# The head of a sketched-attention and ELU kernel: z's sums ahead of the query sketches, the first key transpose ahead of the mask product, one query load

## The chip, the cores and the metric

The kernel runs on one core of a Trainium2 chip. The metric is the device time of one execution, in microseconds (us). Engines are named as the profile names them: PE is the matrix engine (PEld its weight loads), DVE the vector engine, ACT the scalar engine, POOL the GpSimd engine, SP the sync engine, which here only issues DMAs. A "q" behind an engine's name (SPq, ACTq) means its instruction queue, where DMAs are issued.

## The reference

q, k and v are (4, 4, 1088, 32): batch, heads, rows, head size. S1 and S2 are two 8 x 32 sketch matrices.

```
phi(x)  = outer product of (S1 x) and (S2 x), 8 x 8 = 64 features per row
kv      = sum over rows of phi(k) v^T          (64 x 32 per batch and head)
z       = sum over rows of phi(k)              (64 per batch and head)
x       = (phi(q) kv) / (phi(q) z + 1e-6)      -> (4352, 128), heads side by side
h       = x @ w_in                             (128 -> 2048)
out     = elu(h) @ w_out                       (2048 -> 128)
```

The sketches and both weight matrices arrive as 64-bit floats and are rounded to 32 bits on the chip with integer operations (`round_a` to `round_e`). Everything else is 32-bit float.

## The kernel before

**Tiling.** The 1088 rows of a batch are 17 tiles of 64 rows. Keys are handled as two halves u = 0 and 1 of at most nine tiles each (`KT` is 9), which lie in the two halves of the partitions of a result; products for both halves can run side by side in the matrix engine. The 68 tiles of queries are taken in groups of eight tiles (512 rows). Group 0 is the first 512 rows of batch 0, and the head of the kernel is what must happen before group 0 can go through the two large matrix products: sketch the keys of batch 0, build kv and z from them, sketch and normalise the queries of group 0.

**Order.** The schedule is written by hand: each engine executes its instructions in the order of the program text, and an instruction that waits holds all that stand behind it on its engine. Tiles come from rotating buffers, and waits are put in by the framework where data or buffers need them. DMAs are issued from SP and, for the first loads, from ACT. From the ninth on, an issue on SP also waits until an earlier DMA, eight places before it in the order of all issues, has landed.

**The head, in order** (lines of the profile in brackets):

- SP and ACT each load one sketch [L139] and one part of batch 0's keys: SP tiles 0 to 8, ACT tiles 9 to 16, both through `load_hd` [L78]. Then each loads half of group 0's queries [L78 again, called from L144 and L145]. SP goes on with the first weight block [L164], v [L86], the other queries, more weights.
- PE runs `keep_warm` products, whose result is never read [L231]; then the mask product's input `sps` [L265] and `SXps` [L251], then one more unread product with 224 columns [L231].
- DVE multiplies `sps` with a head mask into `Sab`, the sketch matrix spread over heads [L268], and then transposes the keys in four pieces [L244]: tiles 0 to 4 (from SP's load), 9 to 13 (from ACT's load), 5 to 8, 14 to 16. After them come the queries of group 0 [L244].
- `KF(0)`: 18 products of key tiles with `Sab` into two PSUM banks `abp` [L304], and one ACT copy of each bank into `abk` [L312]. The first bank needs tiles i below 5 of both halves, the second the rest.
- `q1_first`: 8 products with the transposed queries, `abqp` [L482], copied by ACT to `abq` [L486].
- `KO_pool` and `KO_first`: the outer products `kp`. POOL makes tiles 0 to 3 [L287], DVE tile 4 and, in one instruction of 1024 elements per partition, tiles 5 to 8 [L374].
- `Z_first`: nine products that sum z over the tiles, `zps` [L382; tiles 0 to 4 need `abk`'s first copy, 5 to 8 its second], an ACT copy `zl` [L404], two products with the masked sketches `SXh` [L226], a DVE mask product that writes the third part of `SW` [L413], and an unread product of 160 columns [L231].
- `q1z_first`: 8 products of the queries with that part of `SW`, `zqp` [L494], which are the queries' denominators before the last reduction.
- `RA(0)` [L103, DVE]: the first step of rounding weight block 0. `RB(0)` is ACT's step of it [L108].
- `q2_den`: DVE multiplies, sums, inverts and scales: `pw` [L569], `den` [L572, L573], `an` [L575]. `q2_out` writes `qp` in two instructions [L586].
- `KA(0)`: 36 products `kv` [L391], and the chain that turns them [L446 to L448]. Then `qp` is transposed on PE [L598], copied by ACT [L599], multiplied with kv [L605], copied to `xg` [L611].
- `mm1_first` and what follows are the first of the large products, `h` [L226], ELU [L791, L793, L799] and `o` [L226], with the rounding of the next weight blocks in between on DVE [L103, L116, L117, L121, L129].

Each product in 32-bit floats is run by PE as two passes, so 18 products show as 36.

From step 2 on a loop over 68 (group, weight block) pairs issues the two large products of each, with the work of the other three batches placed at given steps.

Of the kernel before, what the change touches and what calls it, by code (L numbers as in the profile page):

```python
# [22 lines left out]
def _ap(ap: bass.AP, free):  # L23
    return dataclasses.replace(ap, ap=[list(ap.ap[0])] + [list(x) for x in free])
# [3 lines left out]
def kernel(  # L28
# [21 lines left out]
    nc = tc.nc  # L50
# [7 lines left out]
    NT = S // 64  # L58
    KT = (NT + 1) // 2
# [12 lines left out]
    kT = [const.tile([FD, 2 * KT, 64], F32, name=f"kT{b}") for b in range(2)] * 2  # L72
    qT = [const.tile([FD, NT, 64], F32, name=f"qT{b}") for b in range(2)] * 2

    def load_hd(eng, x, src, b, t0, t1, c=slice(0, 2)):
        if (x, b) not in hd:
            hd[x, b] = work.tile([P, 2, NT, D], F32, name="hd_" + x, tag="hd_" + x)
        eng.dma_start(hd[x, b][:, c, t0:t1, :],  # L78
                      src[b].rearrange("h (a c t) d -> (h a) c t d", a=32, c=2)[:, c, t0:t1, :])
# [61 lines left out]
            eng.dma_start(S16[rs, :], src)  # L141
    load_hd(nc.sync, "k", k, 0, 0, KT)
    load_hd(nc.scalar, "k", k, 0, KT, NT)
    load_hd(nc.sync, "q", q, 0, 0, 8, slice(0, 1))  # L144
    load_hd(nc.scalar, "q", q, 0, 0, 8, slice(1, 2))  # L145
    warm = const.tile([R, 1], F32, name="warm")
    nc.vector.memset(warm[:], 0.0)
    nc.scalar.activation(warm[:], warm[:], EXP)
# [75 lines left out]
    def halves(dst, lhs, rhs, **kw):  # L224
        for u in range(2):
            nc.tensor.matmul(dst[64 * u:64 * u + 64], lhs[:, 64 * u:64 * u + 64], rhs, skip_group_check=True,  # L226
                             tile_position=(0, 64 * u), **kw)

    def keep_warm(n, cols=256):
        for i in range(n):  # L230
            nc.tensor.matmul(idle[:, :cols], some[:, :P], some[:, :cols], skip_group_check=True)  # L231
# [11 lines left out]
    def transp(dst, x, b, t0, t1):  # L243
        nc.vector.transpose(dst[b][:, t0:t1, :].rearrange("p t (a c) -> p c t a", c=2), hd[x, b][:, :, t0:t1, :])  # L244
# [4 lines left out]
    def make_SXh():  # L249
        xps = psum.tile([P, 512], F32, name="SXps", tag="aux")  # L250
        nc.tensor.matmul(xps[:, :FD], idr[:].rearrange("p x j -> p (x j)"), Sx[:].rearrange("p h d -> p (h d)"))  # L251
        nc.scalar.copy(SXh[:], xps[:, :FD])
        nc.gpsimd.tensor_mul(SXh[:].rearrange("p (h d) -> p h d", h=H), SXh[:].rearrange("p (h d) -> p h d", h=H),
                             _ap(hmask[:], [[1, H], [0, D]]))
# [9 lines left out]
    sps = psum.tile([P, 512], F32, name="sps", tag="aux")  # L264
    nc.tensor.matmul(sps[:, :2 * R], Sx[:].rearrange("p h d -> p (h d)"), ident[:, :2 * R])  # L265
    make_SXh()
    keep_warm(1, 224)
    nc.vector.tensor_mul(Sab[:], _ap(sps[:, :2 * R], [[0, H], [1, 2 * R]]), _ap(bmask[:], [[1, H], [0, 2 * R]]))  # L268
    nc.gpsimd.tensor_copy(SW[:, :, :2, :].rearrange("p h x r -> p h (x r)"), Sab[:])

# [26 lines left out]
    def KF(b):  # L297
        ps = [psum.tile([P, 512], F32, name="abp", tag="h", bufs=4) for _ in range(2)]

        part = [(range(5), 0), (range(3), 1)]  # L300
        todo = [(i, u) for r, u in part for i in r] + [x for i in range(5, KT) for x in ((i - 2, 1), (i, 0))]
        todo += [(i, 1) for i in range(KT - 2, KT)]
        for i, u in todo:
            nc.tensor.matmul(ps[i // 5][64 * u:64 * u + 64, 64 * (i % 5):64 * (i % 5) + 64],  # L304
                             kT[b][:, u * KT + i, :], Sab[:].rearrange("p h y -> p (h y)"),
                             skip_group_check=True, tile_position=(0, 64 * u))
        kf_ps.extend(ps)
        ab = feats[b] = work.tile([P, 2, KT, H, R], F32, name="abk", tag="abk", bufs=2)
        for j in range(2):
            t = slice(0, 5) if j == 0 else slice(5, KT)  # L310
            n = t.stop - t.start
            nc.scalar.copy(ab[:, :, t].rearrange("p x t h r -> p x (t h) r"),  # L312
                           ps[j][:, :64 * n].rearrange("p (m x r) -> p x m r", x=2, r=R))
# [49 lines left out]
    def KO_pool():  # L363
        for half in range(2):
            feats[0, half] = work.tile([P, 5, H, R, R], F32, name="kp", tag="kp", bufs=3)
        ab = feats[0][:, :, :4].rearrange("p x t h r -> p (t h) x r")
        outer(feats[0, 0][:, :4].rearrange("p t h i j -> p (t h) i j"), ab, nc.gpsimd)

    def KO_first(t0, t1):
        half, o = divmod(t0, 5)  # L370
        n = t1 - t0
        a_ = kf_ps[half][:, 64 * o:64 * (o + n)].rearrange("p (m x r) -> p m x r", x=2, r=R)[:, :, 1, :]
        b_ = feats[0][:, 0, t0:t1].rearrange("p t h r -> p (t h) r")
        nc.vector.tensor_mul(feats[0, half][:, o:o + n].rearrange("p t h i j -> p (t h) i j"),  # L374
                             _ap(a_, list(a_.ap[1:]) + [[0, R]]), _ap(b_, [[R, n * H], [0, R], [1, R]]))
# [3 lines left out]
    def z_tile(b, ps, i):  # L379
        c = 32 * (i % 4)  # L380
        ab = feats[b]
        nc.tensor.matmul(ps[c:c + 32, R * R:R * R + H * R], ab[:, 0, i].rearrange("p h r -> p (h r)"),  # L382
                         ab[:, 1, i].rearrange("p h r -> p (h r)"), start=(b == 0 and i < 4), stop=(i >= KT - 4),
                         skip_group_check=True, tile_position=(0, c))
# [17 lines left out]
    def ZC(b, ps):  # L402
        zl = work.tile([P, H * R], F32, name="zl", tag="zl")
        nc.scalar.copy(zl[:], ps[:, R * R:R * R + H * R])  # L404
        return zl

    def Z(b, ps, zl):

        halves(ps[:, 96:128], SXh[:], zl[:])

    def Z_out(b, ps):
        z = wzs[b] = SW[:, :, 2, :] if b == 0 else work.tile([FD, H, R], F32, name="wz", tag="wz")[:]
        nc.vector.tensor_mul(z, ps[:, 96:128].rearrange("p (h i) -> p h i", h=H), _ap(bmask[:], [[1, H], [0, R]]))  # L413
# [21 lines left out]
    def Z_first():  # L435
        ps = psum.tile([P, 512], F32, name="zps", tag="h", bufs=4)
        for i in range(KT):
            z_tile(0, ps, i)
        zl = ZC(0, ps)
        Z(0, ps, zl)  # L440
        Z_out(0, ps)
        keep_warm(1, 160)

    def KS_first():
        kd = work.tile([P, 2, R * R], F32, name="kd", tag="kd", bufs=1)
# [18 lines left out]
    def half_tile(g, k):  # L464
        return divmod(8 * g + k, NT)
# [11 lines left out]
    def q1_first():  # L477
        p = psum.tile([P, 512], F32, name="abqp", tag="aux")
        for i in range(4):
            for u in range(2):  # L480
                b, t = half_tile(0, 2 * i + u)
                nc.tensor.matmul(p[64 * u:64 * u + 64, i * 64:i * 64 + 64], qT[b][:, t, :],  # L482
                                 Sab[:].rearrange("p h y -> p (h y)"),
                                 skip_group_check=True, tile_position=(0, 64 * u))
        abw[0] = work.tile([P, H * 4, 2 * R], F32, name="abq", tag="abq", bufs=1)
        nc.scalar.copy(abw[0][:].rearrange("p (h t) y -> p h t y", h=H),  # L486
                       p[:, :256].rearrange("p (t h y) -> p h t y", t=4, h=H))

    def q1z_first():
        p = psum.tile([P, 512], F32, name="zqp", tag="h", bufs=4)  # L490
        for i in range(4):
            for u in range(2):
                b, t = half_tile(0, 2 * i + u)
                nc.tensor.matmul(p[64 * u:64 * u + 64, i * 32:i * 32 + 32].rearrange("p (h r) -> p h r", h=H),  # L494
                                 qT[b][:, t, :], SW[:, :, 2, :], skip_group_check=True, tile_position=(0, 64 * u))
        return p[:, :128].rearrange("p (t h r) -> p h t r", t=4, h=H)
# [349 lines left out]
                eng.dma_start(rows[b, :, t, :], o[64 * u:64 * u + 64, i])  # L846


    for t0, t1 in ((0, 5), (KT, KT + 5), (5, KT), (KT + 5, NT)):
        transp(kT, "k", 0, t0, t1)  # L850
    KF(0)
    transp(qT, "q", 0, 0, 8)
    q1_first()
    KO_pool()
    KO_first(4, 5)
    KO_first(5, KT)
    Z_first()
    zq = q1z_first()
    RA(0)
    q2_den(0, zq)  # L860
# [201 lines left out]
```

## Time and profile before

| | us |
|---|---|
| median of 4 runs | 268.05 |
| lowest and highest of them | 267.55, 268.72 |
| the profiled execution | 267.54 |
| its span, first to last instruction | 265.7 |
| PE busy in it | 259.6 (98%) |
| DVE, ACT, POOL busy | 187.5, 184.0, 159.8 |

The span is counted from the first instruction; about 1.8 us of the execution lie around it. An engine counts as busy from the start to the (for PE modelled) end of its instructions. The waits of an engine are put down to the instruction that released it.

### The profile page before, as it was taken

The page shows a single profiled execution, that of the slowest core. Times are in us where ns is not written, and L with a number is a line of the kernel's source. Part 1 is how long each engine was busy: PE and PEld are TensorE (multiplying, and loading weights), DVE is VectorE, ACT ScalarE, POOL GpSimd, SP SyncE. Part 2 cuts the span into 40 slices and gives each one's busy share as a digit, 9 for nine tenths or more (in the row PEclk, how much of TensorE's full clock was granted, in tenths as well). Part 3 has the DMA queues.
Part 4 walks back from the last instruction along what each step waited for, and adds up shares of the span by engine and source line. Part 5 has one row for each costly group of instructions (what it writes and reads, how often), then busy time and mean ns, then how long its engine had stood idle before and what let it go on. Part 6 is the DMA issues. An engine that isn't in the chain of part 4 may idle for free.

```text
span 265.7 us, 7686 instructions
## 1 busy us (share of the span) xinstructions
PE 259.6 (98%) x3115; PEld 154.4 (58%) x3115; DVE 187.5 (71%) x346; ACT 184.0 (69%) x355; POOL 159.8 (60%) x233
## 2 busy tenths in 40 slices
PE   8899999999999999999999999999999999999994
PEld 6753333343334665668566666666766666666884
DVE  6899999996969796996557766654346444673652
ACT  2379978677566565786577777777777777777782
POOL 4400008204415985798859799898688888898300
PEclk9999999999999999999999999999999999999999
DMA  5999960011002200000100110001000100110011
GB/s 188 316 349 245 272 191 4 0 38 51 0 0 38 47 4 0 2 3 16 28 5 0 22 22 2 0 14 26 9 0 12 31 2 1 18 21 6 2 27 35
DMA packets 26418, 13.60 MB, mean 51 GB/s; under 512 B 19216, under 2 KB 24592, under 8 KB 26384
## 3 DMA queue, kind: packets, MB, share of 16 engines
q1 hardware_dynamic: 25792, 12.66, 18.8%
q8 instruction: 24, 0.39, 0.6%
q10 hardware_dynamic: 592, 0.46, 0.5%
q14 instruction: 10, 0.08, 0.1%
HBM read 10.88 MB, written 2.23 MB: 49 GB/s over the span
## 4 chain that ended last, share of the span: by engine, by line
PE 94%; DVE 4%; issue 1%; ACT 0%; DVEq 0%
PE h L226 43%; PE pb L730 16%; PE pa L730 12%; PE o L226 11%; PE ol L226 3%; PE idle L231 2%; PE kv L391 1%; PE h L648 1%; PE qps L648 1%; DVE qp L586 1%; PE kfps L323 1%; PE qps L542 1%; PE kv L226 1%; PE abp L304 1%; DVE raw L121 0%
## 5 line engine op out<-in xcount | busy, mean ns | idle before, releaser
L799 DVE SCALAR_TENSOR_TENSOR gg<-e,h 128x512 f32<-128x512 f32 (+1 forms) x144 | 92.2, 651 | 64.2 <-ACT e L793 62.9
L226 PE MATMUL h<-xg,W 128*64 128x512 f32 (+1 forms) x584 | 128.7, 563 | 0.0
L791 ACT ACTIVATE e<-h 128x512 f32<-128x512 f32 (+1 forms) x144 | 81.5, 566 | 50.4 <-PE h L226 48.0
L793 ACT ACTIVATE e<-e 128x512 f32<-128x512 f32 (+1 forms) x144 | 87.5, 607 | 4.4
L226 PEld LDWEIGHTS h<-xg,W 128*64 128x64 f32 x584 | 40.1, 137 | 47.4 <-issue 36.8
L710 POOL TENSOR_TENSOR tt<-gg 128x256 f32<-128x256 f32 x48 | 35.2, 732 | 16.4 <-DVE gg L799 16.0
L713 POOL TENSOR_TENSOR tt<-gg 128x256 f32<-128x256 f32 x48 | 35.4, 738 | 14.2 <-DVE gg L799 13.8
L715 POOL TENSOR_TENSOR tt<-gg,tt 128x256 f32<-128x256 f32 x48 | 36.5, 761 | 3.8
L714 POOL TENSOR_TENSOR tt<-tt,gg 128x256 f32<-128x256 f32 x48 | 35.2, 734 | 3.8
L730 PEld LDWEIGHTS pa<-gg,W 128*64 128x64 f32 x384 | 23.6, 137 | 22.8 <-issue 22.1
L226 PE MATMUL o<-gg,W 128*64 128x512 f32 x128 | 30.5, 597 | 0.4 <-DVE W L129 0.4
L730 PE MATMUL pa<-gg,W 128*64 128x128 f32 x384 | 29.5, 274 | 0.0
L730 PE MATMUL pb<-tt,SS 128*64 128x128 f32 x384 | 29.1, 273 | 0.0
L730 PEld LDWEIGHTS pb<-tt,SS 128*64 128x64 f32 x384 | 22.6, 137 | 0.0
L126 POOL TENSOR_TENSOR raw<-raw,tiny 128x512 f32<-128x512 f32 x1 | 1.0, 1047 | 29.9 <-DVE raw L121 29.9
L730 PE MATMUL pb<-gg,SS 128*64 128x128 f32 x192 | 18.7, 273 | 0.0
L730 PE MATMUL pa<-tt,SS 128*64 128x128 f32 x192 | 18.7, 273 | 0.0
L730 PE MATMUL pb<-tt,W 128*64 128x128 f32 x192 | 18.6, 273 | 0.0
L226 PEld LDWEIGHTS o<-gg,W 128*64 128x64 f32 x128 | 8.5, 136 | 16.2 <-issue 13.8
L730 PEld LDWEIGHTS pb<-tt,W 128*64 128x64 f32 x192 | 12.1, 137 | 0.0
L730 PEld LDWEIGHTS pa<-tt,SS 128*64 128x64 f32 x192 | 12.1, 137 | 0.0
L730 PEld LDWEIGHTS pb<-gg,SS 128*64 128x64 f32 x192 | 12.1, 137 | 0.0
(150 smaller groups left out, 243.5 us busy)
## 6 DMA issues: line engine op xcount, KB each, us to landing
raw<-in_moe_w_in_dram SPq DMA_DIRECT2D x8, 256.0 KB, 5.9
raw<-in_moe_w_out_dram SPq DMA_DIRECT2D x8, 256.0 KB, 6.2
hd_k<-in_k_dram SPq DMA_DIRECT2D x3, 544.0 KB, 8.2
hd_q<-in_q_dram SPq DMA_DIRECT2D x3, 544.0 KB, 3.5
v<-in_v_dram SPq DMA_DIRECT2D x4, 288.0 KB, 6.7
out_dram<-ob SPq DMA_DIRECT2D x72, 16.0 KB, 1.5
v<-in_v_dram SPq DMA_DIRECT2D x4, 256.0 KB, 8.2
out_dram<-ob SPq DMA_DIRECT2D x16, 32.0 KB, 1.6
```

What stands on the lines that cost most here:

```text
L226: nc.tensor.matmul(dst[64 * u:64 * u + 64], lhs[:, 64 * u:64 * u + 64], rhs, skip_group_check=True, tile_position=(0, 64 * u), **kw)
L231: nc.tensor.matmul(idle[:, :cols], some[:, :P], some[:, :cols], skip_group_check=True)
L304: nc.tensor.matmul(ps[i // 5][64 * u:64 * u + 64, 64 * (i % 5):64 * (i % 5) + 64], kT[b][:, u * KT + i, :], Sab[:].rearrange("p h y -> p ( ...
L648: nc.tensor.matmul(ps[w][s * r:s * r + s, 64 * k:64 * (k + m)], lhs, qpT[g, i][rows, o + 2 * k:o + 2 * (k + m), f, :], start=(f == 0 and j ...
L710: nc.gpsimd.tensor_tensor(t[:, 0], b12, b11, op=SUB)
L713: nc.gpsimd.tensor_tensor(t[:, 2], b22, b12, op=SUB)
L714: nc.gpsimd.tensor_tensor(t[:, 1], t[:, 2], b11, op=ADD)
L715: nc.gpsimd.tensor_tensor(t[:, 3], b21, t[:, 1], op=SUB)
L730: nc.tensor.matmul(bank[64 * u:64 * u + 64, P * col:P * col + P], lhs, rhs[:, u], start=(first and i in (0, 3)), stop=last, skip_group_che ...
L791: nc.scalar.activation(e, hs[g, cp][c][:, :n], RELU, scale=-1.0)
L793: nc.scalar.activation(e, e, EXP, scale=-1.0)
L799: nc.vector.scalar_tensor_tensor(gs[g, cp][:, c, :n], es[g, cp][:, c, :n], -1.0, hs[g, cp][c][:, :n], op0=ADD, op1=MAX)
```

## The change

Four edits, all in the head:

- the queries of group 0 are loaded whole by one DMA from SP, and ACT issues none for them;
- the transpose of key tiles 0 to 4 stands on DVE ahead of the mask product that makes `Sab`, and the unread product of 224 columns after `SXps` is gone;
- `Z_first` is cut in two. Its nine sums and the copy `zl` stand ahead of `q1_first`, on PE and on ACT; its two products and the mask product stand between the outer products of tiles 5 and 6 and those of tiles 7 and 8, which are now two DVE instructions;
- the unread product after z's products has 96 columns where it had 160.

```diff
-    load_hd(nc.sync, "q", q, 0, 0, 8, slice(0, 1))
-    load_hd(nc.scalar, "q", q, 0, 0, 8, slice(1, 2))
+    load_hd(nc.sync, "q", q, 0, 0, 8)
@@ after make_SXh()
-    keep_warm(1, 224)
+    transp(kT, "k", 0, 0, 5)
     nc.vector.tensor_mul(Sab[:], _ap(sps[:, :2 * R], [[0, H], [1, 2 * R]]), _ap(bmask[:], [[1, H], [0, 2 * R]]))
@@ Z_first
         for i in range(KT):
             z_tile(0, ps, i)
-        zl = ZC(0, ps)
-        Z(0, ps, zl)
-        Z_out(0, ps)
-        keep_warm(1, 160)
+        return ps, ZC(0, ps)
@@ the order of the head
-    for t0, t1 in ((0, 5), (KT, KT + 5), (5, KT), (KT + 5, NT)):
+    for t0, t1 in ((KT, KT + 5), (5, KT), (KT + 5, NT)):
         transp(kT, "k", 0, t0, t1)
     KF(0)
     transp(qT, "q", 0, 0, 8)
+    zps, zl = Z_first()
     q1_first()
     KO_pool()
     KO_first(4, 5)
-    KO_first(5, KT)
-    Z_first()
+    KO_first(5, 7)
+    Z(0, zps, zl)
+    Z_out(0, zps)
+    KO_first(7, KT)
+    keep_warm(1, 96)
     zq = q1z_first()
```

## The prediction

> **What bounds the kernel now.** I read three views of the profiled execution: the page's engine totals, the chain that ended last, and the timeline of the first 22 us.
>
> ```profile
> PE 259.6 (98%) x3115; PEld 154.4 (58%) x3115; DVE 187.5 (71%) x346; ACT 184.0 (69%) x355; POOL 159.8 (60%) x233
> ```
>
> PE is the bound: 98% busy, and in the timeline it never idles after 22.09 us. The first product of `o` there waits for DVE, and before it comes a row of DVE work without holes. The chain that ended last, asked for the first 30 us, shows that row (start, length, what):
>
> ```profile
> 7.53 0.61 PE abqp L482 x16
> 8.16 0.37 ACT abq L486
> 8.54 0.13 ACT zl L404
> 8.80 0.31 PE zps L226 x4
> 9.11 0.47 PE idle L231 x2
> 9.58 0.61 PE zqp L494 x16
> 10.22 0.30 DVE pw L569
> ...
> 11.56 1.29 DVE qp L586 x2
> 12.86 0.69 DVE qT L244
> ...
> 21.61 0.43 DVE W L129
> 22.04 0.04 issue
> 22.09 1.94 PE o L226 x8
> ```
>
> Every piece from 10.22 to 22.04 is DVE's, or a gap of at most 0.1 us between dependent DVE instructions (one piece is booked as "issue" while `qp` still runs). None waits for a DMA. So whatever moves `pw` at 10.22 moves the end by as much. The question is what `pw` waits for, and the timeline answers (start, length, instruction, idle time before it):
>
> ```profile
> 5.08 0.23 DVE L268 TENSOR_TENSOR Sab<-sps,bmask 128x64 f32<-128x64 f32 x1 [0.76 <-PE sps L265]
> 5.39 0.54 PE L231 MATMUL idle<-some 128*128 128x224 f32 x2
> 5.87 1.67 PE L304 MATMUL abp<-Sab,kT 128*64 128x64 f32 x36
> 7.10 0.84 ACT L312 COPY abk<-abp 128x320 f32<-128x320 f32 x2 [1.24 <-PE abp L304]
> 7.44 0.69 PE L482 MATMUL abqp<-Sab,qT 128*64 128x64 f32 x16
> 7.56 1.64 DVE L374 TENSOR_TENSOR kp<-abp,abk 128x256 f32<-128x256 f32 x2 [0.26 <-ACT abk L312]
> 8.06 0.38 PE L382 MATMUL zps<-abk 128*32 128x32 f32 x18
> 8.80 0.31 PE L226 MATMUL zps<-zl,SXh 128*64 128x32 f32 x4 [0.37 <-ACT zl L404]
> 9.22 0.19 DVE L413 TENSOR_TENSOR SW<-zps,bmask 128x32 f32<-128x32 f32 x1
> 9.51 0.66 PE L494 MATMUL zqp<-SW,qT 128*64 128x32 f32 x16
> 10.22 0.29 DVE L569 TENSOR_TENSOR pw<-abq,zqp 128x128 f32<-128x128 f32 x1 [0.51 <-PE zqp L494]
> ```
>
> Read backwards: `pw` waits for `zqp`, `zqp` for `SW`. `SW` has two conditions that come almost together: z's products end at 9.11, and DVE is held by `kp` until 7.56 + 1.64 = 9.20. `kp` wins by some 0.05 us. This closeness decides the forecast.
>
> **The change part by part.** Times below are of the profiled execution, 267.54 us for a span of 265.7, which is 0.5 us under the median 268.05 of the runs.
>
> *The key transposes.* The first needs SP's key load: issued at 1.20, and the DMA list gives 3.7 us to landing, so 4.90. DVE idles 0.76 us before `Sab`, so the transpose starts near 4.92 and, at its 0.50 us, ends at 5.42. Consecutive DVE instructions here start some 0.08 us before their predecessor ends, so `Sab` moves from 5.08 to 5.35 and ends at 5.57, not 5.31. DVE is then free for the second transpose at 5.49, against 5.65 before. But that one reads ACT's load: issued at 1.37, 4.2 us to landing, 5.57. It starts near 5.60, a gain of 0.05. The bounds are 0.16 (landing earlier) and a loss of 0.14, the row of `Sab`'s 0.23 less the overlap, when SP's load lands after 5.2 and `Sab` is held behind a transpose that waits. I take 0.05, by the landing rows.
>
> *The key sketches.* The 18 passes of half u = 1 follow the second transpose 0.15 us behind and 0.058 apart, so they end the sketches. The first sketch, now behind `Sab`, starts at 5.71 instead of 5.87, and is no limit. Both `abk` copies come 0.05 earlier; the second ends at 7.89 (was 7.10 + 0.84 = 7.94).
>
> *z's sums ahead of `abqp`.* This looks like the gain and is not one. The sums of tiles 5 to 8 need the second `abk` copy; they started 0.12 behind it before (8.06) and do so after (8.01). What changes is PE's order: `abqp` ran at 7.44 to 7.96 while PE would have waited for that copy; now it is queued behind the waiting sums. It starts when their last eight passes are through (0.08) and PE has changed to 64-column tiles (0.15, as from `zqp` to `kv` the other way): 8.24. Its 16 passes hold PE for 0.52 us, to 8.76. Meanwhile ACT has made `zl` by 8.52, as no `abq` copy stands ahead of it, and z's products could start 0.14 later, at 8.66. They start at 8.76, behind `abqp`: against 8.80 a gain of only the 0.05 from above. Were the tile change free they would start at 8.66; were it 0.15 longer, at 8.91.
>
> *The outer products cut in two.* This removes DVE's hold: tiles 5 and 6 take 0.69 (the `qp` instruction of the same 512 elements) from 7.92 to 8.61. `SW` then waits for z's products alone: 8.76 + 0.31 + 0.04 = 9.11, against 9.22. The second half runs from 9.22 to 9.91 and `RA(0)` after it, 0.24 to 0.38 long, to 10.07 or 10.20. The cut costs two fixed parts, 2 x 0.69 - 0.08 - 1.23 = 0.07 us. All lies in the 0.51 us that DVE idled before `pw`, leaving it free for `pw` at 10.0 to 10.13. That cover is nearly used up. `RB(0)` on ACT starts 0.4 later, at 10.2, before the `kd` copy at 11.38, and its reader on DVE comes at 13.65. `kv` on PE needs tiles 7 and 8 only in its last eight products, after 10.5; they are ready at 9.91.
>
> *`zqp` and `pw`.* `zqp` starts 0.10 behind `SW` (as 9.41 to 9.51): 9.40. The 96-column product between is through by then, as the 160-column one was. `zqp` ends at 10.06, `pw` starts 0.05 later at 10.11, or with the long `RA(0)` at 10.13. Against 10.22 this is 0.09 to 0.11 earlier; I take 0.10.
>
> *One query load.* SP's half landed at 1.93 + 3.9 = 5.83, ACT's at 2.06 + 4.2 = 6.26; the transpose of them started at 6.63. As one DMA behind SP's keys it carries the same bytes, and even at the landing of the weight block behind it (2.57 + 4.8 = 7.37) the queries would be transposed by 8.1, in time for `abqp` at 8.24. SP's later issues shift by about 0.1 us, while weight block 0 has from 7.4 to 9.8 to spare. ACT's table load, 2.83 to 4.12, starts some 0.7 earlier; its next reader is at 5.59. Cost: nothing. Without that cover it would be one query transpose, 0.67.
>
> *The unread product.* Removed: 0.54 us of PE at 5.39, under which nothing waited. What its lack can do is to the clock. The first unread products run 256 columns per 0.43 us; the same shape at 11.86 takes 0.22. PE's first 4 us thus run at half pace, although the granted clock is shown as 1.00 for that stretch. The removed product's two passes already started 0.19 apart for 224 columns, the full pace. So in this execution the clock had risen before the hole at 5.56 to 5.71 that the removal opens, and holes of 0.37 and 0.39 us at 8.4 and 11.3 were not followed by slow passes. I take 0.
>
> A rule of the Trainium skill speaks against this edit. The page "TensorE: Matmul & The Clock Gate", Part 1, says that the full clock comes after a busy window of about 3.4 us, and that this window runs freely, without regard to the start of the kernel. The row agrees with the first: half pace from 1.19 to about 5.2. The second would mean that another execution can still be slow at 5.6, with the hole inside the window that decides. If the hole spoiled it, the next 3.4 us would be slow and the sum would be a loss of about 1.1 us instead of a gain of 0.10. One trace cannot show how the phase varies.
>
> **The sum.** 0.05 from the transposes and 0.05 from `SW` freed of `kp`: 0.10 us off. 267.54 becomes 267.44, and the median 268.05 becomes 267.95. That is 0.04%, far under the 0.3% (0.8 us) that a measurement of this kernel can tell from no change. By the bounds, `pw` is 0.2 earlier (second transpose at 5.49, then DVE limits) to 0.1 later.
>
> **The rivals.**
>
> 1. *PE's queue eats the gain.* `abqp` holds z's products to 8.91; `SW` comes at 9.26, and all is as before: 268.05, up to 268.15. For it: `abqp` fills the slot z needs. Against it: the tile change has a measured row of 0.15.
> 2. *Slower: the clock rises late.* Place: the hole at 5.56. At half pace the 18 passes of u = 1 are 0.107 apart (0.43 x 64 / 256) instead of 0.058: 0.88 us. `abqp` adds up to 0.34, of which some lies beside waits. About 1.1 in all: 269.05. It decides from the point where the clock is still low at 5.6 and 0.15 us of idle PE keeps it low. Against it: the clock is up by 5.39 in the trace, and 4.2 us of dense products stand ahead.
> 3. *Faster than a measurement needs.* No row holds 0.8 us: even `pw` right behind `RA(0)` gives 0.2. It would take executions in which the clock or the key loads behave otherwise.
> 4. *The loads don't come together as before.* SP's keys land after 5.2, `Sab` is held and `SW` is 0.08 later than before: 268.15.
>
> **How the numbers follow.** The sum as worked out has 0.55, rival 1 0.19, rival 4 0.08; all three lie within 0.3%. The clock rival has 0.06, and the gain beyond the rows 0.05. The rest, 0.07, is scatter: the four runs lie 1.2 us apart, so a median can stray by 0.8, to both sides. Together: faster 0.09, same 0.82, slower 0.09. The range takes the bounds of the sum, 267.85 to 268.15, and about 0.5 us of scatter at each end, a little more below than the rivals need: 267.3 to 268.7. It leaves the clock rival out.
>
> **What the profile after would show.** `Sab` starting near 5.35 and the second transpose near 5.60; `abqp` not before 8.2; `zl` ending near 8.5 with z's products only at about 8.75; `SW` near 9.11, released by PE instead of waiting for `kp`; `pw` near 10.11 with hardly any idle time before it; `o` at 21.98. Wrong would be: z's products well before 8.7 or after 8.9, 64-column passes 0.107 apart after 5.6, or a DVE wait for a DMA between `pw` and `o`.

## The result, and the profile after

The changed kernel takes 267.55 us (median of 54 executions, 267.04 to 269.95) against 267.94 us for the kernel before (78 executions, 267.37 to 270.74): 0.39 us less. The ratio, formed chip by chip, is 0.9981 with a 95% interval of 0.9972 to 0.9990, so 0.51 us less, between 0.27 and 0.75. That is inside the 0.3% called "same", and the sign is the one forecast, but it is four to five times the 0.10 us of the sum.

The page of the profile of the changed kernel (span and engine totals):

```profile
span 265.6 us, 7682 instructions
PE 259.5 (98%) x3113; PEld 155.5 (59%) x3113; DVE 187.5 (71%) x347; ACT 183.9 (69%) x355; POOL 159.7 (60%) x233
```

Its chain that ended last (start, length, what):

```profile
7.87 0.04 issue
7.92 0.27 PE zps L381 x8
8.18 0.62 PE abqp L478 x16
8.80 0.11 PE zps L225 x4
...
9.01 0.19 DVE SW L412
9.20 0.60 DVE kp L373
9.79 0.19 DVE W L103
9.98 0.04 issue
10.03 0.30 DVE pw L565
...
11.37 1.29 DVE qp L582 x2
```

`abqp` now stands in the chain between z's sums and z's products, as foreseen; `kp` and `RA(0)` fill DVE's wait ahead of `pw`. The timeline of the same stretch (lines of the changed kernel):

```profile
4.52 0.51 DVE L243 STREAM_TRANSPOSE kT<-hd_k 128x320 f32<-128x320 f32 x1 [0.39 <-DMA hd_k<-in_k_dram]
4.95 0.18 DVE L267 TENSOR_TENSOR Sab<-sps,bmask 128x64 f32<-128x64 f32 x1
5.34 1.10 DVE L243 STREAM_TRANSPOSE kT<-hd_k 128x320 f32<-128x320 f32 x3 [0.21 <-DMA hd_k<-in_k_dram]
5.40 2.06 PE L303 MATMUL abp<-Sab,kT 128*64 128x64 f32 x36
7.03 0.84 ACT L311 COPY abk<-abp 128x320 f32<-128x320 f32 x2 [1.25 <-PE abp L303]
7.50 0.68 PE L381 MATMUL zps<-abk 128*32 128x32 f32 x18
8.63 0.26 PE L225 MATMUL zps<-zl,SXh 128*64 128x32 f32 x4
9.01 0.19 DVE L412 TENSOR_TENSOR SW<-zps,bmask 128x32 f32<-128x32 f32 x1 [0.42 <-PE zps L225]
10.03 0.29 DVE L565 TENSOR_TENSOR pw<-abq,zqp 128x128 f32<-128x128 f32 x1
```

Here is the first surprise. The keys landed earlier than in the trace of before (the transposes start at 4.52 and 5.34, not at the 4.92 and 5.60 of my working), and the key sketches are slow: 36 passes in 2.06 us instead of 1.67. In the kernel before the last three transposes, the second one first, stood here:

```profile
5.65 1.06 DVE L244 STREAM_TRANSPOSE kT<-hd_k 128x320 f32<-128x320 f32 x3
```

The trace's clock record (when PE's full pace begins and ends; it has no entry before that, where the views print 1.00) has PE at full pace from 6.33 us in this execution; in the profile of before it is 5.32. Below, this moment is called the rise. Until it the 64-column passes of one half stand 0.107 us apart, from it on 0.058. So the two profiles, 0.12 us apart (267.54 and 267.42), compare an earlier clock with a later one. `pw` is 0.19 earlier and `o` is too (22.09 to 21.90).

### The profile page after: what moved, and what is told of

It reads as the page before. It is cut to its first block, busy times and chain, and to the rows that moved or that the text cites. A ratio compares the mean times of both kernels' runs of the same rounds, so it can differ in the third digit from the quotient of the medians.

```text
span 265.6 us, 7682 instructions
## 1 busy us (share of the span) xinstructions
PE 259.5 (98%) x3113; PEld 155.5 (59%) x3113; DVE 187.5 (71%) x347; ACT 183.9 (69%) x355; POOL 159.7 (60%) x233
## 4 chain that ended last, share of the span: by engine, by line
PE 93%; DVE 5%; issue 1%; ACT 0%; DVEq 0%
PE h L225 43%; PE pb L726 16%; PE pa L726 12%; PE o L225 11%; PE ol L225 3%; PE kv L390 1%; PE idle L230 1%; PE h L644 1%; PE qps L644 1%; DVE qp L582 1%; PE abp L303 1%; PE kfps L322 1%; PE qps L538 1%; PE kv L225 1%; DVE raw L121 0%
## 5 line engine op out<-in xcount | busy, mean ns | idle before, releaser
L225 PEld LDWEIGHTS h<-xg,W 128*64 128x64 f32 x584 | 41.0, 137 | 46.6 <-issue 37.2
```

## The experiments

Five theories run through the expectations. P is the prediction. T says that the transposes were worth more than 0.05, since the landing I took was a late one. Z says that z's sums ahead of `abqp` do bring something. N says that the removed product itself costs time when it is met at half pace. L asks whether the one query load is behind the landings. Two more, C and D, belong to one run each and are told there. All ratios are to the kernel before on the same chip, with 95% intervals. What tells the theories apart is mostly the trace, as most intervals are 0.2 to 0.3% wide.

### The kernel before again, and the loads

`before_again` has no edit.

> The kernel before, unchanged, timed against itself: ratio 1.000. It is here for its single executions. Theory C (the moment at which PE's clock rises explains the spread): executions whose mean granted clock is below 1.000 rose early (the clock also falls a fixed stretch later, just before the end) and should be about 0.4 us faster than those at 1.000, as in the changed kernel (267.2 against 267.6). Rival (spread is DMA or chance): no difference between the two groups.

Measured: 1.0004 (0.9988 to 1.0020). Theory C failed on this kernel: of the other 35 executions of it on that chip, 20 with a mean clock under 1.000 have a median of 267.93, 15 with 1.000 one of 267.97. In the changed kernel 22 with less have 267.24 and 32 with 1.000 have 267.62. The mean clock is thus a poor label, and the traces show one reason: it falls short of 1.000 when PE's clock falls before the end of the span, and in the two traces with the earliest rise (4.14 and 4.41) the fall lies behind the end, so that they count as 1.000 (last section). The rise in each trace is the better label. The run's own trace has it at 4.90, `pw` at 10.08.

`load_alone`:

```diff
-    load_hd(nc.sync, "q", q, 0, 0, 8, slice(0, 1))
-    load_hd(nc.scalar, "q", q, 0, 0, 8, slice(1, 2))
+    load_hd(nc.sync, "q", q, 0, 0, 8)
```

> The kernel before with the queries of group 0 loaded whole by SP, and nothing else changed. Theory P (my prediction): costs and brings nothing, 1.000, keys of ACT's load transposed from 5.6 as before. Theory L (without ACT's query DMA the keys land earlier: 4.49 and 5.32 in the changed kernel's trace against 4.87 and 5.54): landings near 4.5 and 5.3; the first transpose stays behind the mask product at 5.2, so at most 0.1 us, ratio 0.9996 to 1.000.

Measured: 0.9995 (0.9985 to 1.0005), and keys at 4.49 and 5.16. The DMA lists of `before_again` and then `load_alone` (bytes, us from issue to landing; the issues are at 1.20 and 1.37):

```profile
hd_k<-in_k_dram SPq DMA_DIRECT2D x1, 288.0 KB, 3.5
hd_k<-in_k_dram ACTq DMA_DIRECT2D x1, 256.0 KB, 4.0
```

```profile
hd_k<-in_k_dram SPq DMA_DIRECT2D x1, 288.0 KB, 3.3
hd_k<-in_k_dram ACTq DMA_DIRECT2D x1, 256.0 KB, 3.8
```

The second transpose still starts at 5.51, since it stands behind `Sab` and the first one. The load alone brings nothing that can be told, as both theories had it.

`two_loads` is the changed kernel with the edit above undone.

> The changed kernel with the two query loads of before. Theory P: as the changed kernel, ratio 0.998 to 0.999. Theory L: keys land at 4.9 and 5.5 again, the second transpose starts at 5.6 instead of 5.34, and some 0.2 us of the gain is lost: ratio 0.999 to 1.000.

Measured: 0.9980 (0.9966 to 0.9995): nothing lost. Its keys landed at 4.61 and 5.28, its second transpose started at 5.30. Theory L finds no support as a source of the gain: the trace is not as it had it (5.5 and 5.6), though the interval (up to 0.9995) reaches into its 0.999 to 1.000. Over all fourteen traces ACT's keys landed at 5.28 to 5.54 with two query loads (six traces, mean 5.39) and at 5.13 to 5.41 with one (eight, mean 5.24): 0.16 us earlier, with overlap. The landing that I took my 5.57 from, 5.54, is the latest of the fourteen.

### The edits one at a time

`keys_first` is the kernel before with:

```diff
-    keep_warm(1, 224)
+    transp(kT, "k", 0, 0, 5)
...
-    for t0, t1 in ((0, 5), (KT, KT + 5), (5, KT), (KT + 5, NT)):
+    for t0, t1 in ((KT, KT + 5), (5, KT), (KT + 5, NT)):
```

> The kernel before with one edit: the first key transpose ahead of the mask product, and the 224-column product gone. Theory P (the prediction's term for the transposes): the second transpose waits for its load and gains 0.05, so 0.05 us, ratio 0.9998. Theory T (the five traces so far show ACT's keys landed at 5.16 to 5.54, 5.32 in the middle, so the transpose can start at 5.2 to 5.4, where before it stood behind the mask product at 5.5 to 5.65): it gains 0.2 to 0.3, and as both the sums and the outer products hang on it, pw comes 0.2 to 0.3 earlier: ratio 0.9990 to 0.9993.

Measured: 0.9997 (0.9982 to 1.0012), which decides nothing. The trace decides for T: the second transpose starts at 5.38 and `pw` at 10.00, with two query loads and a rise only at 6.12.

```profile
5.15 0.19 DVE L268 TENSOR_TENSOR Sab<-sps,bmask 128x64 f32<-128x64 f32 x1
5.38 1.10 DVE L244 STREAM_TRANSPOSE kT<-hd_k 128x320 f32<-128x320 f32 x3
8.59 0.31 PE L226 MATMUL zps<-zl,SXh 128*64 128x32 f32 x4 [0.37 <-ACT zl L404]
9.00 0.19 DVE L413 TENSOR_TENSOR SW<-zps,bmask 128x32 f32<-128x32 f32 x1
10.00 0.29 DVE L569 TENSOR_TENSOR pw<-abq,zqp 128x128 f32<-128x128 f32 x1 [0.46 <-PE zqp L494]
```

`z_cut` is the kernel before with the third and fourth edits:

```diff
-        zl = ZC(0, ps)
-        Z(0, ps, zl)
-        Z_out(0, ps)
-        keep_warm(1, 160)
+        return ps, ZC(0, ps)
...
+    zps, zl = Z_first()
     q1_first()
     KO_pool()
     KO_first(4, 5)
-    KO_first(5, KT)
-    Z_first()
+    KO_first(5, 7)
+    Z(0, zps, zl)
+    Z_out(0, zps)
+    KO_first(7, KT)
+    keep_warm(1, 96)
```

> The kernel before with one edit: the cut of z's work and of the outer products (sums ahead of the query sketches, 96-column product). Theory P: z's products are held by the query sketches, only SW's wait for kp goes: 0.05, ratio 0.9998. Theory Z (in the changed kernel z's products start 0.76 us behind the second copy of the key sketches, before 0.86 to 0.95): z's products themselves come 0.1 to 0.15 earlier and pw 0.1 to 0.2: ratio 0.9993 to 0.9996. Neither edit alone reaches the changed kernel's 0.998 in theories T and Z; their sum does.

Measured: 0.9995 (0.9984 to 1.0005). In its trace one of the two query loads landed at 7.50 (elsewhere by 6.26) and cost nothing, as `abqp` started only at 8.67: the slack that the prediction gave the queries is there. Z's products start 0.77 us behind the second `abk` copy, as in every kernel with this cut, and `pw` 1.40 us behind them. The two links, over the traces of both orders:

| | order of before: before, before_again, load_alone, keys_first, no_product | z cut: after, two_loads, product_back, cut_at_8, z_cut |
|---|---|---|
| end of second `abk` to z's products | 0.86, 0.95, 0.74, 0.82, 0.96 | 0.77, 0.76, 0.76, 0.77, 0.77 |
| z's products to `pw` | 1.41, 1.41, 1.41, 1.41, 1.41 | 1.40, 1.40, 1.40, 1.40, 1.40 |

So the order of z's work brings 0.10 us on the mean, between nothing (`load_alone`) and 0.20 (`no_product`), and the outer products cut in two, with all behind them, 0.01.

### The unread product

`product_back` is the changed kernel with `keep_warm(1, 224)` put back ahead of the first transpose.

> The changed kernel with the unread 224-column product put back behind SXps. Theory P: nothing, as in the changed kernel, ratio 0.998. Rival N (the removal is part of the gain, since PE at half pace spends 0.37 us on that product and the key sketches then start late): first key sketch at 5.75 or later instead of 5.4, pw up to 0.2 later, ratio 0.9985 to 0.9990, most in executions whose clock rises after 5.7.

Measured: 0.9984 (0.9971 to 0.9997), near the changed kernel. Its profiled execution had the earliest clock of the kernels with the first transpose moved, 4.41, and PE is at full pace for all of its key sketches, as in the two traces of the kernel before. So it shows the gain of the other edits there:

```profile
4.86 0.54 PE L230 MATMUL idle<-some 128*128 128x224 f32 x2
5.25 1.10 DVE L243 STREAM_TRANSPOSE kT<-hd_k 128x320 f32<-128x320 f32 x3
5.34 1.74 PE L304 MATMUL abp<-Sab,kT 128*64 128x64 f32 x36
9.65 0.29 DVE L566 TENSOR_TENSOR pw<-abq,zqp 128x128 f32<-128x128 f32 x1
```

`pw` at 9.65 is 0.43 and 0.57 earlier than in the two traces of the kernel before, whose clocks rose at 4.90 and 5.32.

`no_product` is the kernel before without that product and nothing else.

> The kernel before with one edit: the 224-column product left out. Two traces of kernels with that product whose clock rose late (7.1 and 6.4) show the first key sketch 0.61 us behind the first key transpose's end, since PE was still at that product at half pace; the changed kernel's with a rise at 6.3 starts its sketches at 5.40. Theory N: the first sketch follows the transpose by 0.14 also in a late execution, those gain 0.2 to 0.4 and early ones nothing; ratio 0.9990 to 0.9996. Theory P (the product costs nothing): 1.000, sketches no earlier.

Measured: 0.9991 (0.9982 to 1.0001), with executions from 267.35 to 268.01 where the kernel before, beside it, spread from 267.33 to 269.24: the low end is unmoved and the high end is gone, which fits N. Its trace rose early (4.14) and can't show it, but it shows something else. With so early a clock `Sab` is there at 4.68, and the second transpose starts at 5.36, just behind its landing (5.33), in the old order too. So moving the first transpose has little left to gain there:

```profile
4.68 0.23 DVE L267 TENSOR_TENSOR Sab<-sps,bmask 128x64 f32<-128x64 f32 x1 [0.55 <-PE sps L265]
5.36 0.84 DVE L244 STREAM_TRANSPOSE kT<-hd_k 128x320 f32<-128x320 f32 x2
9.97 0.29 DVE L568 TENSOR_TENSOR pw<-abq,zqp 128x128 f32<-128x128 f32 x1 [0.61 <-PE zqp L493]
```

Two traces with the product and a late rise do show it, `load_alone` (7.08) and `z_cut` (6.38). `load_alone`:

```profile
5.08 1.48 DVE L243 STREAM_TRANSPOSE kT<-hd_k 128x320 f32<-128x320 f32 x4
5.31 0.95 PE L230 MATMUL idle<-some 128*128 128x224 f32 x2
6.20 1.85 PE L303 MATMUL abp<-Sab,kT 128*64 128x64 f32 x33
10.79 0.29 DVE L568 TENSOR_TENSOR pw<-abq,zqp 128x128 f32<-128x128 f32 x1 [0.38 <-PE zqp L493]
```

The product takes 0.95 us and the key sketches start at 6.20, though the first keys were transposed by 5.59.

To meet the half pace in every execution, three runs leave out the unread products at the very start:

```diff
-    keep_warm(3)
-    keep_warm(1, 128)
```

`late_clock` and `late_clock_2` are the changed kernel with this; `late_product` has the 224-column product put back as well.

> The changed kernel without the unread products ahead of the mask product's input (three of 256 columns, one of 128), so that PE starts at 4.3 us instead of 1.2 and its clock must rise some 3 us later in every execution: this measures by itself the price of a late clock, rival 2 of the prediction. By its working: about 1.1 us over the changed kernel, ratio to before 1.002 to 1.003, KF's passes 0.107 apart. Rival (the head hides half pace, since it is bound by waits): under 0.4 us, ratio below 1.000.

> late_clock again, beside late_product on the same chip: ratio 1.0018 as before, pw near 10.9, key sketches from 5.6.

> The changed kernel without the unread products ahead of the mask product's input, as in late_clock, and with the 224-column product put back: the clock is late in every execution, so that the product is met at half pace every time. Theory N: the product takes 0.37 us or more there and holds the key sketches, which start at about 6.0 instead of 5.58: 0.2 to 0.4 us over late_clock (here again as late_clock_2). Theory P: no difference to it.

Measured: 1.0018 (1.0005 to 1.0031), 1.0033 (1.0012 to 1.0054) and 1.0038 (1.0024 to 1.0052). A late clock thus costs the changed kernel about 1 us and more (0.9981 to 1.0018 and 1.0033), as rival 2 had priced it (1.1), with the passes 0.107 apart as it had them; here the clock is late because PE starts late, not because of a hole. The times don't separate the product from its lack. The traces do: `late_clock_2`, then `late_product`:

```profile
4.95 0.22 DVE L265 TENSOR_TENSOR Sab<-sps,bmask 128x64 f32<-128x64 f32 x1
5.45 2.88 PE L301 MATMUL abp<-Sab,kT 128*64 128x64 f32 x36
10.90 0.29 DVE L563 TENSOR_TENSOR pw<-abq,zqp 128x128 f32<-128x128 f32 x1
```

```profile
5.11 0.23 DVE L266 TENSOR_TENSOR Sab<-sps,bmask 128x64 f32<-128x64 f32 x1
5.47 0.95 PE L230 MATMUL idle<-some 128*128 128x224 f32 x2
6.36 2.88 PE L302 MATMUL abp<-Sab,kT 128*64 128x64 f32 x36
11.82 0.29 DVE L564 TENSOR_TENSOR pw<-abq,zqp 128x128 f32<-128x128 f32 x1
```

The sketches start 0.50 behind the start of `Sab` without the product (in `late_clock` too) and 1.25 with it, both run 2.88 us, and `pw` is 0.91 later (10.94 in `late_clock`, so 0.88 against that). Of the 0.91, 0.75 is the product; `Sab` itself came 0.16 later in that execution. N holds in the traces, at more than its 0.2 to 0.4, where the clock is still low when PE comes to the product. They are single executions (268.31, 268.32 and 269.20 us), and the times of the others do not confirm so much.

### Two tries at more

`cut_at_8`:

```diff
-    KO_first(5, 7)
+    KO_first(5, 8)
...
-    KO_first(7, KT)
+    KO_first(8, KT)
```

> The changed kernel with the outer products cut behind tile 7 instead of tile 6 (1 tile after SW instead of 2). In the changed kernel's trace pw at 10.03 starts right behind RA(0), which ends at 9.995, while its product zqp ended at 9.91: DVE is the last to release it. Theory D: with 0.27 us less DVE work behind SW, pw starts 0.05 us behind zqp, 0.07 earlier, and SW is not held, as tiles 5 to 7 end at about 8.9: 0.07 us, not to be told in the time (0.9978), but in the trace. Rival: SW is held by the longer first part, pw as late or later.

Measured: 0.9994 (0.9984 to 1.0004). Theory D falls: `RA(0)` was done at 9.69, `zqp` at 9.87, and `pw` started at 9.98, 0.12 behind `zqp` as in the changed kernel (9.91 to 10.03). The trace shows what else comes:

```profile
9.98 0.29 DVE L565 TENSOR_TENSOR pw<-abq,zqp 128x128 f32<-128x128 f32 x1 [0.30 <-PE zqp L490]
10.68 1.21 PE L390 MATMUL kv<-kp,v 128*32 128x64 f32 x72 [0.81 <-DMA v<-in_v_dram]
```

The `kv` products waited 0.81 us for a half of v that landed at 10.54 in this execution. In the changed kernel's profile it was 0.15 us, for a landing at 9.93; in the kernel before they waited for nothing. SP issues this half of v behind the whole query load, at 3.89 instead of 3.72; it landed at 9.54 to 10.54 with one query load (mean 9.97) and at 9.46 to 10.27 with two (9.74).

`queries_after_z` moves `q1_first()` from ahead of `Z` to behind it and leaves out `keep_warm(1, 96)`.

> The changed kernel with the query sketches moved on PE from ahead of z's products to behind them, in place of the 96-column product, which is left out. In the traces z's products start 0.19 us behind the copy zl where PE stands at the query sketches, 0.15 where it waits. Theory: z's products, SW and pw 0.04 earlier, zqp not held, as the sketches' 0.5 us fit between; ratio 0.998 as the changed kernel, the difference to be told in the trace alone (pw 2.13 us behind the second copy of the key sketches instead of 2.17). Rival: the sketches reach into zqp's start and pw comes later.

Measured: 0.9996 (0.9984 to 1.0007). Z's products started 0.72 behind the second `abk` copy instead of 0.77, but took 0.31 us instead of 0.26, and `pw` came 2.16 behind that copy, as in `two_loads`. Nothing gained; no version here beats the changed kernel.

## Why the prediction was right, and where its size was off

**Right:** the path. From `pw` to `o` DVE takes 11.86 to 11.91 us in all fourteen traces, whenever `pw` comes, so the head's gain reaches `o` in full. Right too: z's products stand behind `abqp`, which holds them a little (they start 0.05 behind its last pass, at 8.63), and the profiled time (267.44 forecast, 267.42 found). That last agreement is luck, as two different clocks stand behind it. For the median the sum was out by 0.40 (267.95 forecast, 267.55 found).

One sign named for being wrong did show: from 5.6 to 6.2 the sketches' passes stood 0.107 apart in the changed kernel's profile. The sketches took 0.39 us longer than before, but they started 0.47 earlier (5.40 against 5.87), so that rival 2's loss did not come with it.

**The transposes** were mis-sized, at 0.05: 5.34 in place of 5.60 for the second one. I took ACT's landing from one execution, which was the latest of fourteen. Over the traces the second transpose starts at 5.51 to 5.66 in four of the five with the old order (mean 5.58) and at 5.15 to 5.43 in the nine with the first transpose moved (mean 5.29). The term is 0.29, near twice the upper bound of 0.16 that I had set, since part of it is the keys' earlier landing. With the fifth, `no_product` and its very early clock (5.36), the old order's mean is 5.54 and the term 0.25.

**The query load** "costs nothing" held in time. That it brings nothing was not quite so: keys 0.16 earlier on the mean. Alone it moves no transpose; beside the moved transpose it can, but `two_loads` shows no loss without it. Its price, which I left out, is v: issued 0.17 later, with `kv` waiting for it in three traces (below).

**z's sums ahead of `abqp`** are worth 0.10, not nothing. The step that failed is "0.12 behind the copy": in the changed kernel the last eight passes start 0.05 behind it (7.86 to 7.92). The 0.12 before was PE's change of tiles behind `abqp`, not the wait for the copy. In the five traces of the old order the sums start 0.15 behind the last pass of `abqp`, whether the copy ended 0.21 before (`no_product`) or 0.01 after (`load_alone`). And as the last sums start earlier, `abqp` follows at 8.11, not at 8.24 or "not before 8.2".

**`SW` freed of `kp`** was a misreading. `SW` starts 0.11 to 0.13 us behind the end of z's products in all fourteen traces, in the kernel before too (9.11 to 9.22, 8.97 to 9.08), and a DVE instruction held only by its predecessor starts some 0.08 before that one ends. So PE held it, not `kp`; that `kp` ended 0.02 us before `SW` was a coincidence. (`load_alone` alone, with 0.13, has `SW` 0.08 before the end of `kp`, held by it, for 0.02.) The 0.05 booked here has to be taken out; the order of z's work gave it back.

**The unread product** was taken at nothing, as work "under which nothing waited", and I saw the risk in its absence. That step holds only where the clock is up. A late clock makes the product itself long: 0.95 us for two passes that take 0.54, right ahead of the key sketches, which then wait for it. The hole that its removal leaves did no visible harm: with the hole the clock rose at 4.14 and 5.86 to 6.74 in six traces, without it at 4.41 to 7.08 in five (the three runs with the late start of PE left aside).

Here the Trainium skill, "TensorE: Matmul & The Clock Gate", Part 1, agrees with the runs: its free-running window is seen as a rise anywhere between 4.14 and 7.08 us in eleven traces, 2.9 us wide against its 3.4. I had cited it as a danger to the change; the same fact works for it.

**The sum, at equal clocks.** `pw` by the moment of the rise:

| rise | old order of the transposes | first transpose moved, z cut |
|---|---|---|
| 4.1 to 5.3 | 9.97 (4.14, no_product), 10.08 (4.90), 10.22 (5.32) | 9.65 (4.41, product_back) |
| 5.8 to 6.0 | | 9.94 (5.86, two_loads), 9.98 (5.96, cut_at_8) |
| 6.3 to 6.4 | 10.59 (6.38, z_cut) | 10.03 (6.33, after) |
| 7.1 | 10.79 (7.08, load_alone) | |

Early, 0.29 + 0.10 + 0.01 = 0.40 is expected from the terms above, and 0.43 and 0.57 are seen against the kernel before. Against `no_product` it is 0.32: 0.11 from the transposes, 0.20 from z's order and 0.01. Later the product adds its share: at 6.3 to 6.4 the gap is 0.56 although `z_cut` has z's gain already; the second transpose accounts for 0.31 of it (5.66 to 5.34). The other 0.24 I put down to the product, as what is left. Not all of a gain arrives: `o` to the end takes 243.62 us in both traces of before, 243.71 in the changed kernel, 243.96 in `product_back` and 244.13 in `cut_at_8`. In the last three PE stood idle ahead of `kv` (0.15, 0.61 and 0.81 us), with v landing at 9.93, 10.01 and 10.54. I had weighed `kv` against the outer products and forgotten v: a wait that takes the place of the one removed. `keys_first`, with `o` at 21.88 like `cut_at_8` but without the wait, has 243.69. The wait is not all, though, since `keys_first`, `no_product` (243.70) and `queries_after_z` (243.84) lose behind `o` without it. With some 0.1 given back, the 0.39 to 0.51 us in the times is in keeping with the traces. No single edit's ratio is clear of 1 by its interval; those of the changed kernel, `two_loads` and `product_back`, which have the moves of the transpose and of z's work together, are; those of their variants `cut_at_8` and `queries_after_z` are not.

Open: what gives back the 0.1 to 0.2 us behind `o` where v was in time, and how often the clock rises late, and so how the timed gain divides between the product and the rest. The intervals of `no_product` and `product_back` are too wide for it, and the mean clock of an execution is too coarse a label.

## What to carry to other kernels

A start that hangs on loads and on a clock which rises at a varying moment has to be compared over several traces: one profile gave me the latest landing of fourteen and a rise at 5.32, the second an earlier landing and a rise at 6.33. An instruction that starts just behind its predecessor is not thereby held by it; compare the start with each possible releaser in a second trace, since the true one keeps its distance. And products that only keep PE busy are not free ahead of work that waits for them: while the clock is low they take nearly twice as long (0.95 us against 0.54), and that is when they are in the way.

## What the runs showed that I had not expected

- A second engine to wait for can cost 0.07 us. `pw` starts 0.05 us behind `zqp` in the five traces of the old order (10.17 to 10.22 before) and 0.12 in the nine with z's work cut (9.91 to 10.03 after). There ACT's copy `abq` has become a second thing that `pw` waits for, and the trace has an event-semaphore instruction for `zqp` ahead of it on DVE's queue. It costs only when the wait that ends last is the one in that extra instruction: of the other DVE instructions that waited over 0.15 us for ACT, in either trace, 38 have such an instruction ahead but end their wait with their own semaphore, 0.03 behind ACT, as those without it do, and 31 that end it with the extra one start 0.09 behind.
- The shorter unread product and z's shorter products (0.26 us instead of 0.31) give about as much back. `zqp` starts 0.05 behind `SW` instead of 0.10: the product of 160 columns had held it, against my "through by then". In the old order `zqp` starts 0.40 behind the end of z's products in all five traces, in `load_alone` too, where `SW` came 0.02 later.
- PE's clock falls 259.41 us after it rose in twelve of the fourteen traces (5.32 and 264.73 before, 6.33 and 265.74 after), and 262.83 after it in the two with the earliest rise, `no_product` and `product_back`: 3.41 us more. Each time this is 2.2 to 5.3 us behind the last product.
